# Halves exchanged on ScalarE, and a second layer whose two weight parts pass TensorE as one operand

## The chip, the cores and the metric

The kernel runs on one core of a Trainium2 chip. The time is the device time of one execution in microseconds (us). Three runs of the kernel before gave 2334.14, 2334.78 and 2337.91 us; their median, 2334.78 us, is the time before. One further execution was profiled, and every row quoted below is from that one.

The core's engines are named as the profile names them: PE is TensorE's matmul, PEld its weight load, DVE is VectorE, ACT is ScalarE, POOL is GpSimd, SP is SyncE (here the queue that starts most DMA transfers). PSUM is the memory that PE's matmuls write; the kernel uses it as eight banks of 512 float32 columns each.

## The reference

```python
X = np.fft.rfft(x, axis=1)                       # x: 8 batches, 2496 positions, 256 columns
y = np.fft.irfft(X * F[None], n=2496, axis=1)    # F = filt_r + i filt_i: a global filter
# mixture of experts on the 19968 rows of y: the two best of 8 experts for each row
noisy = x @ w_gate + np.log1p(np.exp(x @ w_noise)) * noise
for e in range(8):
    for k in range(2):                           # rows whose k-th choice is expert e
        h = np.maximum(x[mask] @ w1[e], 0.0)     # 256 -> 1024
        out[mask] += top2_w[mask, k, None] * (h @ w2[e])   # 1024 -> 256
```

Each row passes two experts, so 39936 rows pass the two layers. All of it is float32.

## The kernel before

**The filter.** The transform of a batch is cut into small matrix products (39 by 64 points) over two column halves; `n` counts the halves of all batches, so n = 2 and 3 are the second batch. For each n there are five groups `kg`. `kg1` (line 382 on) multiplies a group by a fixed matrix into a PSUM bank `q3`, and then applies the complex filter: partitions 0 to 63 hold real parts, 64 to 127 imaginary parts. DVE forms `a = p3 * fr` (L397), `b[0:64] = p3[64:128] * fi[64:128]` (L398) and `b[64:128] = p3[0:64] * fi[0:64]` (L399), so the halves change places in the two multiplications that write b. Then a and b are added, on POOL for n below 4 and on DVE afterwards (L400). `kg2` (L413) is the inverse transform of a on PE. The first two batches go through this at the start, in an order that is written out by hand (the list `plan`, kept on each engine by `pin`), together with the gating of the first batch (`gate`, `route`, lines 711 to 925).

**The experts.** `expert` (line 1047 on) works on blocks of 512 rows, four tiles t of 128 rows, and at the end on 18 units of 256 rows, two tiles each. A block belongs to one expert. `gather` fetches its rows from `y` by index (POOL, L977), `turn` transposes them on PE (L993). In the first layer PE computes `hps` for eight slices f of the 1024 hidden columns, ACT applies the relu into `hh` (L1075) and DVE computes the rest, `hl` (L1076). In the second layer PE adds up, for each tile t, the eight slices into `yps`; ACT scales the result by the gate into a row of `stage` (L1100), and POOL adds it to the output by index (L1101).

**Two parts of each number.** After the first stage the operands of matmuls have the type `float32r`, and every operand is split into a high part, rounded to that type, and the rest: weights w1 and w2 in `wsplit` (ACT copies the high part, L1037, DVE subtracts, L1038), activations as `hh` and `hl`. A product then takes three matmuls, which `_mm3` issues at lines 120, 121 and 122: high by high, high by rest, rest by high.

```python
def _mm3(nc, o, lh, ll, rh, rl, start=True, stop=True):
    nc.tensor.matmul(o, lh, rh, start=start, stop=False)
    nc.tensor.matmul(o, lh, rl, start=False, stop=False)
    nc.tensor.matmul(o, ll, rh, start=False, stop=stop)
```

The first operand is loaded into the array (the weight load of PE, 128 by 128), the second streams past it: 512 columns in the first layer, 256 in the second. There the loaded operand is `hh` or `hl`, and the streamed one is `w2h` or `w2l`.

**PSUM.** Of the eight banks two are under the tag `hps`, two under `yps`, one `xps`, three `fps` for the filter. Every third slice of the first layer (f = 2 and 5) uses a `yps` bank too. In the second layer two tiles t share one `yps` bank, each with half of its columns.

**What sets the order.** The order of instructions on each engine is made when the program is built, by a list scheduler that has its own estimate of durations; each engine then runs its list strictly in that order, and semaphores make it wait for the others. `ready` in `expert` is the number of batches whose transform must be complete before a block is taken: the block of batch i has ready = i + 1. From `FIRST` and `PAIRS`, two blocks are taken with ready 1, ten with ready 2 and two with ready 3; all others have ready 4 or more. The filter work of later batches is woven between the blocks.

Of the kernel before, what the change touches and what calls it, by code (L numbers as in the profile page):

```python
# [10 lines left out]
F32 = mybir.dt.float32  # L11
R32 = mybir.dt.float32r
# [3 lines left out]
ALU = mybir.AluOpType  # L16
# [113 lines left out]
PACES = 115  # L130
FILL = {0: 0, 1: 14}
RAW = 3
FIRSTS = 2
EARLY = {"q1": "hps", "q2": "hps", "q5": "yps", "q6": "yps", "u1": "xps"}
BANKS = {"hps": 2, "yps": 2, "xps": 1, "fps": 3}
# [4 lines left out]
class Moe:  # L140
# [165 lines left out]
    def s1(self, bt, g0):  # L306

        nc, P = self.nc, self.P
        if g0 == 0:
            self.Fd[bt] = self.dp.tile([3 * NG, CB, D], F32, name="fd", bufs=2)  # L310
        x = self.xx.pop((bt, g0))
        if self.early and bt < RAW:

            q = self.ps("q1")[:120]
            nc.tensor.matmul(q, self.rC, x, start=True, stop=True)  # L315
            return self.s1e(bt, g0, q)
        xh = P.tile([RP, 512], R32, name="xh", **(dict(tag="w2h", bufs=4) if self.early else dict(bufs=1)))
        xl = P.tile([RP, 512], R32, name="xl", **(dict(tag="w2l", bufs=4) if self.early else dict(bufs=1)))
        nc.scalar.copy(xh, x)
        nc.vector.tensor_sub(xl, x, f32v(xh))  # L320
        q = self.ps("q1")[:120]
        Ch, Cl = self.cC
        nc.tensor.matmul(q, Ch, xh, start=True, stop=False)  # L323
        nc.tensor.matmul(q, Cl, xh, start=False, stop=False)
        nc.tensor.matmul(q, Ch, xl, start=False, stop=True)
        self.s1e(bt, g0, q)
# [54 lines left out]
    def kg1(self, n, kg):  # L381
# [6 lines left out]
        else:  # L388
            nc.tensor.matmul(p, Mh, th, start=True, stop=False)
            nc.tensor.matmul(p, Mh, tl, start=False, stop=False)  # L390
            nc.tensor.matmul(p, Ml, th, start=False, stop=True)
        a = P.tile([128, 4, 128], F32, name="a", **(dict(tag="w2h", bufs=4) if self.early else dict(bufs=2)))
        b = P.tile([128, 4, 128], F32, name="b", **(dict(tag="w2l", bufs=4) if self.early else dict(bufs=1)))
        p3 = p.rearrange("p (k d) -> p k d", k=4)
        fr = self.fr[:, h, 4 * kg:4 * kg + 4]
        fi = self.fi[:, h, 4 * kg:4 * kg + 4]
        nc.vector.tensor_mul(a, p3, fr)  # L397
        nc.vector.tensor_mul(b[0:64], p3[64:128], fi[64:128])  # L398
        nc.vector.tensor_mul(b[64:128], p3[0:64], fi[0:64])  # L399
        (nc.gpsimd if n < 4 else nc.vector).tensor_add(a, a, b)  # L400
        self.zz[n, kg] = a

    def kg2(self, n, kg):
# [627 lines left out]

    def wsplit(self, st, nm, q):
        nc, P = self.nc, self.P
        h = P.tile([128, 2, 256], R32, name=nm + "h", bufs=4)
        l = P.tile([128, 2, 256], R32, name=nm + "l", bufs=4)
        sv = st.rearrange("p (k f) -> p k f", k=2)
        nc.scalar.copy(h, sv)  # L1037
        nc.vector.tensor_sub(l, sv, f32v(h))  # L1038
        return h, l

    def fetch(self, may):

# [5 lines left out]
    def expert(self, parts, may, fill=None):  # L1048
# [5 lines left out]
        while self.ahead:  # L1054
# [33 lines left out]
            yield  # L1088
            for t in range(nt):

                if t % 2 == 0:
                    bank = self.PS.tile([128, 2, D], F32, name="yps", bufs=2)
                p = bank[:, t % 2]
                for f in range(8):
                    h, l = hh[f]
                    wh, wl = w2[f // 2]
                    _mm3(nc, p, h[:, t * 128:(t + 1) * 128], l[:, t * 128:(t + 1) * 128], wh[:, f % 2], wl[:, f % 2],
                         start=(f == 0), stop=(f == 7))
                o = self.slot("yo")
                nc.scalar.activation(o, p, AF.Copy, scale=gate[:, t])  # L1100
                a = nc.gpsimd.indirect_dma_start(  # L1101
                    out=self.io["out"][:BLK + ready * ROWS], out_offset=bass.IndirectOffsetOnAxis(ap=ids[:, t:t + 1], axis=0),
                    in_=o, in_offset=None, compute_op=ALU.add)
# [113 lines left out]
```

## Time and profile before

| | |
|---|---|
| runs | 2334.14, 2334.78, 2337.91 us |
| profiled execution | 2338.18 us, of which the span of its instructions 2336.4 us |
| PE busy | 2282.7 us (98%), 15201 matmuls |
| weight loads busy | 2015.8 us (86%) |
| DVE, ACT, POOL busy | 1442.4 us (62%), 1180.1 us (51%), 942.4 us (40%) |
| DMA | 329.88 MB, mean 141 GB/s |
| granted TensorE clock, mean | 0.993 |

A row of the timeline gives start and duration in us, engine, line, operation, what is written and read, its shape, and how many neighbours it merges; behind it in brackets stands the idle time of the engine before it and what ended that. In a list of groups a row gives the number of instructions, their busy time, the mean of one in ns, and the idle time before them. The end of a matmul is modelled in this profile, so the time of one matmul is read here from the distance between starts, not from its printed duration.

### The profile page before, as it was taken

What the parts mean: (1) busy time and instruction counts of PE and PEld (TensorE: products, weight loads), DVE (VectorE), ACT (ScalarE), POOL (GpSimd) and SP (SyncE); (2) the same over time, 40 slices, a digit from 0 to 9 for tenths busy, and PEclk for the clock granted to TensorE, in tenths of its full rate; (3) what the DMA queues carried; (4) which work ended last, traced back from release to release, by engine and by line L of the source; (5) the groups of instructions that cost most, each with busy time, mean ns of one, the idle gap of its engine ahead of it and who ended that gap; (6) DMA issues with size and microseconds to landing.
All of it is one profiled execution on the core that took longest, in us unless ns stands there. A gap on an engine that the chain in (4) does not pass through costs nothing.

```text
span 2336.4 us, 43304 instructions
## 1 busy us (share of the span) xinstructions
PE 2282.7 (98%) x15201; PEld 2015.8 (86%) x15201; DVE 1442.4 (62%) x3067; ACT 1180.1 (51%) x2353; POOL 942.4 (40%) x837
## 2 busy tenths in 40 slices
PE   8779999999999999999999999999999999999998
PEld 6448888888888888888888888888989898999998
DVE  4967798778669555765558654844343435456775
ACT  6356656654554454444544444444343435456775
POOL 4214244332434333443344333444444444445452
PEclk9989999999999999999999999999999999999999
DMA  8587757765655555455454553344444435567774
GB/s 236 162 244 201 194 139 200 178 157 121 179 133 146 123 123 133 113 145 119 112 118 102 129 140 84 89 99 98 85 94 89 98 84 130 125 162 219 221 224 100
DMA packets 284737, 329.88 MB, mean 141 GB/s; under 512 B 37371, under 2 KB 197603, under 8 KB 284515
## 3 DMA queue, kind: packets, MB, share of 16 engines
q1 hardware_dynamic: 222435, 241.61, 34.5%
q0 software_dynamic: 62080, 85.47, 21.5%
q8 instruction: 121, 1.98, 0.4%
q14 instruction: 101, 0.83, 0.1%
HBM read 221.98 MB, written 105.78 MB: 140 GB/s over the span
## 4 chain that ended last, share of the span: by engine, by line
PE 91%; DVE 4%; DMA 2%; ACT 1%; issue 1%; POOL 0%; SPq 0%; POOLq 0%; ACTq 0%; DVEq 0%
PE yps L122 13%; PE yps L120 13%; PE yps L121 13%; PE hps L120 12%; PE hps L121 12%; PE hps L122 12%; PE xps L993 3%; PE q L413 3%; PE q L477 1%; PE u L424 1%; PE q L500 1%; PE q L315 1%; PE q L502 1%; PE q L501 1%; PE q L323 1%
## 5 line engine op out<-in xcount | busy, mean ns | idle before, releaser
L120 PE MATMUL yps<-w2h,hh 128*128 128x256 f32 x2560 | 725.7, 286 | 0.8 <-ACT stage L1100 0.6
L121 PE MATMUL yps<-w2l,hh 128*128 128x256 f32 x2560 | 716.6, 283 | 0.0
L122 PE MATMUL yps<-w2h,hl 128*128 128x256 f32 x2560 | 706.9, 283 | 0.3 <-DVE hl L1076 0.3
L1076 DVE SCALAR_TENSOR_TENSOR hl<-hps,hh 128x512 fp32r<-128x512 f32 (+1 forms) x712 | 439.1, 631 | 354.1 <-ACT hh L1075 352.7
L1101 POOL DMA_INDIRECT out<-stage,ids x320 | 532.4, 1664 | 202.7 <-ACT stage L1100 127.6
L977 POOL DMA_INDIRECT stage<-y,ids x320 | 323.1, 1010 | 705.3 <-PE xps L993 343.5
L121 PE MATMUL hps<-mxl,w1h 128*128 128x512 f32 (+1 forms) x1424 | 529.4, 373 | 0.0
L122 PE MATMUL hps<-mxh,w1l 128*128 128x512 f32 (+1 forms) x1424 | 526.5, 372 | 0.0
L120 PE MATMUL hps<-mxh,w1h 128*128 128x512 f32 (+1 forms) x1424 | 519.6, 378 | 5.5 <-DVE hl L1076 3.7
L120 PEld LDWEIGHTS yps<-w2h,hh 128*128 128x128 f32 x2560 | 485.7, 190 | 15.1 <-ACT stage L1100 0.8
L122 PEld LDWEIGHTS yps<-w2h,hl 128*128 128x128 f32 x2560 | 482.1, 191 | 11.9 <-issue 1.7
L1075 ACT ACTIVATE hh<-hps 128x512 fp32r<-128x512 f32 (+1 forms) x712 | 382.5, 555 | 216.8 <-PE hps L122 205.3
L121 PEld LDWEIGHTS yps<-w2l,hh 128*128 128x128 f32 x2560 | 485.9, 191 | 6.5
L1100 ACT ACTIVATE stage<-yps,gt 128x256 f32<-128x256 f32 x320 | 147.2, 477 | 330.8 <-PE yps L122 321.1
L122 PEld LDWEIGHTS hps<-mxh,w1l 128*128 128x128 f32 x1424 | 267.4, 188 | 45.8
L120 PEld LDWEIGHTS hps<-mxh,w1h 128*128 128x128 f32 x1424 | 264.6, 189 | 48.8 <-DVE hl L1076 5.9
L121 PEld LDWEIGHTS hps<-mxl,w1h 128*128 128x128 f32 x1424 | 268.0, 188 | 34.7
L998 DVE TENSOR_TENSOR mxl<-xps,mxh 128x512 fp32r<-128x512 f32 (+1 forms) x178 | 113.1, 636 | 145.2 <-ACT mxh L997 142.8
L997 ACT CAST mxh<-xps 128x512 fp32r<-128x512 f32 (+1 forms) x178 | 96.8, 544 | 197.1 <-PE xps L993 163.2
L1038 DVE TENSOR_TENSOR w2l<-stage,w2h 128x512 fp32r<-128x512 f32 x216 | 140.8, 686 | 51.2 <-ACT w2h L1037 48.9
L1037 ACT CAST w1h<-stage 128x512 fp32r<-128x512 f32 x180 | 111.6, 621 | 108.8 <-PE hps L121 70.3
L1038 DVE TENSOR_TENSOR w1l<-stage,w1h 128x512 fp32r<-128x512 f32 x180 | 123.5, 686 | 60.7 <-ACT w1h L1037 57.3
(207 smaller groups left out, 2470.9 us busy)
## 6 DMA issues: line engine op xcount, KB each, us to landing
stage<-w SPq DMA_DIRECT2D x396, 256.0 KB
x<-x SPq DMA_DIRECT2D x88, 256.0 KB
fd<-c SPq DMA_DIRECT2D x77, 240.0 KB
wb<-w SPq DMA_DIRECT2D x18, 1024.0 KB
fx<-fd SPq DMA_DIRECT2D x140, 128.0 KB
out<-z SPq DMA_DIRECT2D x24, 702.0 KB
y<-yt SPq DMA_DIRECT2D x40, 248.6 KB
y<-yt SPq DMA_DIRECT2D x40, 234.0 KB
```

What stands on the lines that cost most here:

```text
L120: nc.tensor.matmul(o, lh, rh, start=start, stop=False)
L121: nc.tensor.matmul(o, lh, rl, start=False, stop=False)
L122: nc.tensor.matmul(o, ll, rh, start=False, stop=stop)
L977: self.pin(lambda: self.nc.gpsimd.indirect_dma_start(out=x, out_offset=None, in_=self.y[:BLK + ready * ROWS], in_offset=bass.IndirectOffse ...
L997: nc.scalar.copy(h, q[:, :w])
L998: nc.vector.tensor_sub(l, q[:, :w], f32v(h))
L1037: nc.scalar.copy(h, sv)
L1038: nc.vector.tensor_sub(l, sv, f32v(h))
L1075: nc.scalar.activation(h, p, AF.Relu)
L1076: nc.vector.scalar_tensor_tensor(l, p, 0.0, f32v(h), op0=ALU.max, op1=ALU.subtract)
L1100: nc.scalar.activation(o, p, AF.Copy, scale=gate[:, t])
L1101: a = nc.gpsimd.indirect_dma_start(out=self.io["out"][:BLK + ready * ROWS], out_offset=bass.IndirectOffsetOnAxis(ap=ids[:, t:t + 1], axis= ...
```

## The change

Two places change, and the buffers of the first stage that go with them.

First, for n = 2 and 3 `kg1` has ACT copy the two halves of the bank crosswise into b (two copies of 64 by 512, L405 and L406 of the changed kernel); DVE then computes a = p3 * fr (L407), b = b * fi over all 128 partitions (L408), and a - b (L409). No addition is left on POOL there.

Second, the high part and the rest of w2 lie in one tile `hl` of shape 128 x 2 x 2 x 256. Where ready is at least 4, one matmul streams both parts past `h`, 512 columns, into a whole bank (L1119), and a second one adds the product of `l` and the high part to its first half (L1120). The second half of the bank is added at the end, by a DVE instruction that multiplies it by the gate and adds it to what ACT has written into `stage` (L1126). Each tile t takes a bank of its own there. Below ready 4 the three matmuls stay.

```diff
+WIDE = 4
@@ s1
-        xh = P.tile([RP, 512], R32, name="xh", **(dict(tag="w2h", bufs=4) if self.early else dict(bufs=1)))
-        xl = P.tile([RP, 512], R32, name="xl", **(dict(tag="w2l", bufs=4) if self.early else dict(bufs=1)))
+        xh = P.tile([RP, 512], R32, name="xh", bufs=1)
+        xl = P.tile([RP, 512], R32, name="xl", bufs=1)
@@ kg1
-        a = P.tile([128, 4, 128], F32, name="a", **(dict(tag="w2h", bufs=4) if self.early else dict(bufs=2)))
-        b = P.tile([128, 4, 128], F32, name="b", **(dict(tag="w2l", bufs=4) if self.early else dict(bufs=1)))
+        if self.early:
+            ab = P.tile([128, 2, 4, 128], F32, name="ab", tag="w2", bufs=4)
+            a, b = ab[:, 0], ab[:, 1]
+        else:
+            a = P.tile([128, 4, 128], F32, name="a", bufs=2)
+            b = P.tile([128, 4, 128], F32, name="b", bufs=1)
...
-        nc.vector.tensor_mul(a, p3, fr)
-        nc.vector.tensor_mul(b[0:64], p3[64:128], fi[64:128])
-        nc.vector.tensor_mul(b[64:128], p3[0:64], fi[0:64])
-        (nc.gpsimd if n < 4 else nc.vector).tensor_add(a, a, b)
+        if 2 <= n < 4:
+            nc.scalar.copy(b[0:64], p3[64:128])
+            nc.scalar.copy(b[64:128], p3[0:64])
+            nc.vector.tensor_mul(a, p3, fr)
+            nc.vector.tensor_mul(b, b, fi)
+            nc.vector.tensor_sub(a, a, b)
+        else:
+            nc.vector.tensor_mul(a, p3, fr)
+            nc.vector.tensor_mul(b[0:64], p3[64:128], fi[64:128])
+            nc.vector.tensor_mul(b[64:128], p3[0:64], fi[0:64])
+            (nc.gpsimd if n < 4 else nc.vector).tensor_add(a, a, b)
@@ wsplit
-        h = P.tile([128, 2, 256], R32, name=nm + "h", bufs=4)
-        l = P.tile([128, 2, 256], R32, name=nm + "l", bufs=4)
+        if nm == "w2":
+            hl = P.tile([128, 2, 2, 256], R32, name="w2", bufs=4)
+            h, l = hl[:, 0], hl[:, 1]
+        else:
+            h = P.tile([128, 2, 256], R32, name=nm + "h", bufs=4)
+            l = P.tile([128, 2, 256], R32, name=nm + "l", bufs=4)
...
-        return h, l
+        return hl if nm == "w2" else (h, l)
@@ expert
-                if t % 2 == 0:
+                wide = ready >= WIDE
+                if wide or t % 2 == 0:
                     bank = self.PS.tile([128, 2, D], F32, name="yps", bufs=2)
-                p = bank[:, t % 2]
+                p = bank[:, 0 if wide else t % 2]
                 for f in range(8):
-                    h, l = hh[f]
-                    wh, wl = w2[f // 2]
-                    _mm3(nc, p, h[:, t * 128:(t + 1) * 128], l[:, t * 128:(t + 1) * 128], wh[:, f % 2], wl[:, f % 2],
-                         start=(f == 0), stop=(f == 7))
+                    h, l = (a[:, t * 128:(t + 1) * 128] for a in hh[f])
+                    hl = w2[f // 2][:, :, f % 2]
+                    if wide:
+                        nc.tensor.matmul(bank, h, hl, start=(f == 0), stop=False)
+                        nc.tensor.matmul(p, l, hl[:, 0], start=False, stop=(f == 7))
+                    else:
+                        _mm3(nc, p, h, l, hl[:, 0], hl[:, 1], start=(f == 0), stop=(f == 7))
                 o = self.slot("yo")
                 nc.scalar.activation(o, p, AF.Copy, scale=gate[:, t])
+                if wide:
+                    nc.vector.scalar_tensor_tensor(o, bank[:, 1], gate[:, t], o, op0=ALU.mult, op1=ALU.add)
```

The lists of the engines move at three places that matter below. In their rows a name with a number is one buffer, and the brackets name the engines whose semaphores the instruction waits for.

PE, a late block of four tiles, at the first matmul of the third tile that it evicts. Before:

```order
L122 MATMUL hps_22100<-mxh1_21971,w1l_21938 128x512
L121 MATMUL hps_22111<-mxl1_21972,w1h_21937 128x512
L122 MATMUL hps_22111<-mxh1_21971,w1l_21938 128x512
L993 MATMUL xps_22204<-ident_70,stage_83 128x128 [waits DMASW4_49,PE_49]
L993 MATMUL xps_22204<-ident_70,stage_83 128x128 [waits DMASW5_49]
L993 MATMUL xps_22204<-ident_70,stage_83 128x128 [waits DMASW6_49]
L993 MATMUL xps_22204<-ident_70,stage_83 128x128 [waits DMASW7_49]
L120 MATMUL yps_21977<-w2h_21615,hh_21834 128x256 [waits Activation_49]
L121 MATMUL yps_21977<-w2l_21616,hh_21834 128x256
L122 MATMUL yps_21977<-w2h_21615,hl_21835 128x256
L120 MATMUL yps_21977<-w2h_21615,hh_21845 128x256
L121 MATMUL yps_21977<-w2l_21616,hh_21845 128x256
```

And with the change, the same place of the same block:

```order
L122 MATMUL hps_20806<-mxh1_20703,w1l_20670 128x512
L121 MATMUL hps_20817<-mxl1_20704,w1h_20669 128x512
L122 MATMUL hps_20817<-mxh1_20703,w1l_20670 128x512
L1007 MATMUL xps_20906<-ident_70,stage_83 128x128 [waits DMASW4_49,PE_49]
L1007 MATMUL xps_20906<-ident_70,stage_83 128x128 [waits DMASW5_49]
L1007 MATMUL xps_20906<-ident_70,stage_83 128x128 [waits DMASW6_49]
L1007 MATMUL xps_20906<-ident_70,stage_83 128x128 [waits DMASW7_49]
L1119 MATMUL yps_20749<-w2_20377,hh_20566 128x512 [waits DVE_49]
L1120 MATMUL yps_20749<-w2_20377,hl_20567 128x256
L1119 MATMUL yps_20749<-w2_20377,hh_20577 128x512
L1120 MATMUL yps_20749<-w2_20377,hl_20578 128x256
L1119 MATMUL yps_20749<-w2_20402,hh_20588 128x512
```

The third tile starts behind the same work. Before, it took the other half of the first tile's bank (yps_21977), and waited for ACT, which had to have read the first half; now it takes the whole bank of the first tile, and waits for DVE, which reads last.

DVE in the same block, before and then with the change:

```order
L1076 SCALAR_TENSOR_TENSOR hl_21912<-hps_21904,hh_21911 128x512 [waits Activation_49]
L998 TENSOR_TENSOR mxl1_21972<-xps_21966,mxh1_21971 128x512 [waits Activation_49]
L1076 SCALAR_TENSOR_TENSOR hl_22108<-hps_22100,hh_22107 128x512 [waits PE_49,Activation_49]
L1076 SCALAR_TENSOR_TENSOR hl_22119<-hps_22111,hh_22118 128x512 [waits PE_49,Activation_49]
L1038 TENSOR_TENSOR w2l_22123<-stage_83,w2h_22122 128x512 [waits DMAHW6_49,Activation_49]
```

```order
L1095 SCALAR_TENSOR_TENSOR hl_20644<-hps_20636,hh_20643 128x512 [waits Activation_49]
L1012 TENSOR_TENSOR mxl1_20704<-xps_20698,mxh1_20703 128x512 [waits Activation_49]
L1126 SCALAR_TENSOR_TENSOR stage_83<-yps_20709,gt_20473,stage_83 128x256 [waits Activation_49]
L1126 SCALAR_TENSOR_TENSOR stage_83<-yps_20729,gt_20473,stage_83 128x256 [waits Activation_49]
L1126 SCALAR_TENSOR_TENSOR stage_83<-yps_20749,gt_20473,stage_83 128x256 [waits Activation_49]
L1095 SCALAR_TENSOR_TENSOR hl_20814<-hps_20806,hh_20813 128x512 [waits PE_49,Activation_49]
L1095 SCALAR_TENSOR_TENSOR hl_20825<-hps_20817,hh_20824 128x512 [waits PE_49,Activation_49]
```

Three of the new additions stand between the rest of the transposed rows (`mxl1`) and the next two `hl`.

DVE at the end of the first stage, at the last group of the second batch. Before, with POOL's addition on its own list, and then with the change:

```order
L397 TENSOR_TENSOR a<-q_1168,fr 128x512 [waits PE_49,Pool_49]
L398 TENSOR_TENSOR b<-q_1168,fi 64x512
L399 TENSOR_TENSOR b<-q_1168,fi 64x512
L902 TENSOR_TENSOR oc<-oc,half 117x224 [waits DVE_49]
L910 TENSOR_TENSOR rx<-rx,ra 128x56 [waits PE_49]
L910 TENSOR_TENSOR rx<-rx,ra 128x56 [waits DVE_49,PE_49]
```

```order
L407 TENSOR_TENSOR ab<-q_1158,fr 128x512 [waits PE_49,Activation_49]
L408 TENSOR_TENSOR ab<-ab,fi 128x512
L924 TENSOR_TENSOR rx<-rx,ra 128x56 [waits PE_49]
L409 TENSOR_TENSOR ab<-ab 128x512 [waits DVE_49]
L924 TENSOR_TENSOR rx<-rx,ra 128x56 [waits DVE_49,PE_49]
```

DVE has three instructions of the group as before, but its first one now waits for ACT's two copies, since all of them write the one tile `ab`.

## The prediction

> **What bounds the kernel now.** I read the page's busy shares first, then the busy time by stretch, then who waits for whom, and last the timeline of PE alone.
>
> ```profile
> PE 2282.7 (98%) x15201; PEld 2015.8 (86%) x15201; DVE 1442.4 (62%) x3067; ACT 1180.1 (51%) x2353; POOL 942.4 (40%) x837
> PE 91%; DVE 4%; DMA 2%; ACT 1%; issue 1%; POOL 0%; SPq 0%; POOLq 0%; ACTq 0%; DVEq 0%
> ```
>
> PE is busy for 98% of the span, and the chain that ended last runs through PE for 91%. The Trainium skill ("Perfetto Trace Analysis", section "Identifying the Most-Contended Engine") says that the busy share of matmuls is a poor measure, since matmuls overlap, and points to the weight loads; these are at 86% here, so the trace agrees that PE is the engine to look at.
>
> A windows view splits the span at the end of the first stage, at the first wide block and at the first small unit. Its columns are the stretch and its length, then busy us and instructions for PE, PEld, DVE, ACT and POOL, granted clock, DMA share and GB/s. The second fence is the list of PE's waits after 622 us (total us, times, longest).
>
> ```profile
> 0.00:200.00 200.00, 162.83 (x868) 106.72 (x869) 138.80 (x408) 101.31 (x200) 51.62 (x55) 0.94 0.73 210
> 622.00:2120.00 1498.00, 1495.92 (x9842) 1336.27 (x9841) 830.21 (x1671) 691.12 (x1337) 628.33 (x547) 1.00 0.50 116
> 2120.00:2336.00 216.00, 206.70 (x1740) 206.23 (x1738) 148.47 (x305) 144.78 (x341) 97.59 (x93) 0.99 0.68 188
> ```
>
> ```profile
> PE hps L120 <- DVE hl L1076: 1.7, 4, 1.0
> PE yps L120 <- ACT stage L1100: 0.6, 1, 0.6
> ```
>
> After 622 us PE waits 2.3 us in all. There the time is what PE needs to issue its list; a shorter list shortens the run one for one as long as no new wait comes. Only the first 200 us, with 37 us of idle PE, are bound by other things.
>
> **What a matmul costs.** Printed durations overlap, so I take the distance between starts. First row and last of a run of first-layer matmuls (512 columns), then of second-layer ones (256 columns):
>
> ```profile
> 2093.09 0.39 PE L120 MATMUL hps<-mxh,w1h 128*128 128x512 f32 x1
> ...
> 2098.43 0.40 PE L122 MATMUL hps<-mxh,w1l 128*128 128x512 f32 x1
> 2324.40 0.28 PE L121 MATMUL yps<-w2l,hh 128*128 128x256 f32 x1
> ...
> 2327.03 0.28 PE L122 MATMUL yps<-w2h,hl 128*128 128x256 f32 x1
> 1806.10 0.28 PE L120 MATMUL yps<-w2h,hh 128*128 128x256 f32 x1
> ...
> 1808.26 0.28 PE L120 MATMUL yps<-w2h,hh 128*128 128x256 f32 x1
> ```
>
> The first run has 23 steps in 5.34 us, 232.2 ns each. The others have 22 steps in 2.63 us and 18 in 2.16 us, 119.5 and 120.0 ns; I use 119.6. Two matmuls of 256 columns take 239.2 ns, one of 512 takes 232.2: what a matmul costs besides its columns is 7.0 ns (6.8 to 7.8 by the two runs). That, and not a third of the work, is what the change can save, because the columns streamed stay the same.
>
> **The change, part by part.** How many are wide: evictions of tiles by stretch, where the kernel's rule puts 56 (14 blocks of four) below ready 4.
>
> ```profile
> 0.00:622.00 622.00, 25.82 (x56) 0.98 0.68 185
> 622.00:2120.00 1498.00, 104.30 (x228) 1.00 0.50 116
> 2120.00:2336.00 216.00, 17.09 (x36) 0.99 0.68 188
> ```
>
> 228 tiles (57 blocks) and 36 (18 units of two) are wide, 264 in all, with eight slices each: 2112 times three matmuls become two. Per slice 3 x 119.6 = 358.8 ns become 232.2 + 119.6 = 351.8. In all 2112 x 7.0 = **14.8 us off PE**.
>
> This prices the wide matmul as a first-layer one of the same width. It differs in one thing that no row shows: its streamed operand is two pieces of 256, 512 elements apart. If a second piece cost what a second matmul costs, it would take 239.2 and PE would gain nothing; at the other end, single steps of that run print as 0.23 or 0.24, so none is below 225 ns, and 2112 x 14.2 ns would be 30 us. I take 232.2, the mean of the nearest rows.
>
> What the additions cost, and the operations of `kg1`:
>
> ```profile
> L1100 ACT ACTIVATE stage<-yps,gt 128x256 f32<-128x256 f32 x320 | 147.2, 477 | 330.8 <-PE yps L122 321.1 <-DMA stage<-y,ids 3.5 <-ACT stage L1100 1.5
> L1076 DVE SCALAR_TENSOR_TENSOR hl<-hps,hh 128x256 fp32r<-128x256 f32 x144 | 57.2, 418 | 18.5 <-ACT hh L1075 18.5
> L397 DVE TENSOR_TENSOR a<-q,fr 128x512 f32<-128x512 f32 x80 | 54.7, 684 | 21.4 <-PE q L391 11.5 <-PE q L387 6.4 <-PE q L349 2.9
> L400 DVE TENSOR_TENSOR a<-a,b 128x512 f32<-128x512 f32 x60 | 41.1, 685 | 0.4
> L400 POOL TENSOR_TENSOR a<-a,b 128x512 f32<-128x512 f32 x20 | 26.1, 1303 | 67.2 <-DVE b L399 50.0 <-DVE st L841 12.1 <-PE q L387 2.6
> L414 ACT COPY G<-q 128x512 f32<-128x512 f32 x80 | 46.9, 587 | 73.1 <-PE q L413 72.7
> ```
>
> A new addition has the form of the 128 x 256 `hl` row, 0.42 us. 264 of them are 110 us of DVE; between 622 and 2120 us they raise it from 830 of 1498 us (55%) to 926 (62%), and the small units from 69% to 76%. DVE stays well below PE, so its total costs nothing. What can cost is the handing over of a bank: the third tile of a block, which waited for ACT, now waits for DVE behind ACT. The same place in the trace:
>
> ```profile
> 1802.53 0.69 DVE L998 TENSOR_TENSOR mxl<-xps,mxh 128x512 fp32r<-128x512 f32 x1 [2.46 <-ACT mxh L997]
> 1803.12 0.84 ACT L1100 ACTIVATE stage<-yps,gt 128x256 f32<-128x256 f32 x2 [0.63 <-PE yps L122]
> 1805.67 0.36 PE L120 MATMUL yps<-w2h,hh 128*128 128x256 f32 x1
> ```
>
> ACT has read the first tile at about 1803.6 (half of the merged row, 0.48). DVE is free since 1803.22, so the addition would end at 1803.6 + 0.05 + 0.42 = 1804.1. PE comes to the third tile at 1805.67, 1.6 us later, and in the new list some 0.23 earlier, since one first-layer matmul less stands between. 1.3 us of cover remain. The fourth tile has more: a tile of 2.8 us lies between. If the cover went, each 1 us of lateness would cost 57 us. I set **1 us** for the new waits, from the places where filter work lies on DVE ahead of an addition; bounds 0 and 15 us.
>
> At the end of the run:
>
> ```profile
> 2324.18 0.38 PE L120 MATMUL yps<-w2h,hh 128*128 128x256 f32 x1 [0.61 <-ACT stage L1100]
> 2327.35 0.47 ACT L1100 ACTIVATE stage<-yps,gt 128x256 f32<-128x256 f32 x1 [3.22 <-PE yps L122]
> 2328.10 1.56 POOL L1101 DMA_INDIRECT out<-stage,ids  x1 [1.95 <-ACT stage L1100]
> ```
>
> The last tile waited 0.61 us for ACT because it shared a bank; with a bank of its own it doesn't: **-0.6 us**. Between the last L1100 and the last L1101 an addition of 0.42 and a handing over of 0.05 come in: **+0.5 us**.
>
> `kg1`, ten groups. DVE has three instructions of 0.68 as before (2.05 us): the multiplication over all partitions takes what L397 or L400 on DVE takes. POOL loses 10 x 1.3 us. ACT gains 20 copies; L414's 0.59 for as many columns is my estimate for each, 12 us, on an engine that is half idle in the first 200 us. On the way of one group POOL's 1.3 us goes away, and ACT's 1.2 us comes ahead of DVE. Which of them shows is told by the last group:
>
> ```profile
> 105.00:115.00 10.00, 8.87 (x63) 5.28 (x64) 9.80 (x22) 2.34 (x5) 3.27 (x3) 0.83 0.23 59
> 112.32 1.10 PE L387 MATMUL q<-fx,cm 128*128 128x512 f32 x2
> 116.51 0.68 DVE L397 TENSOR_TENSOR a<-q,fr 128x512 f32<-128x512 f32 x1
> 118.76 1.27 POOL L400 TENSOR_TENSOR a<-a,b 128x512 f32<-128x512 f32 x1 [3.29 <-DVE b L399]
> 119.74 0.42 PE L913 MATMUL ra<-ident,rx 128*56 128x128 f32 x1 [0.31 <-DVE rx L910]
> 120.08 2.08 PE L413 MATMUL q<-cf,a 128*128 128x128 f32 x8
> ```
>
> DVE is busy 9.80 of 10 us and comes to the group at 116.51, 3 us after its matmul (112.32 plus 1.10): ACT's copies fit in that time. PE stands at L913 until 120.16, which is bound by DVE's `rx`, so POOL's end at 120.03 is not what delays L413. DVE's amount is unchanged, so I take **0**; bounds -1.4 (POOL's leg was the late one after all) and +3 us (DVE meets five of the groups before ACT is done, and waits 0.6 us, one copy, in each).
>
> **Sum.** 2338.2 (the profiled execution) - 14.8 + 1 - 0.6 + 0.5 + 0 = 2324.3. That execution stands 3.4 us above the median of the runs, 2334.78, so for a median of runs I predict 2324.3 - 3.4 = **2321 us**, 0.6% faster. 0.2%, 4.7 us, is about what a measurement of this kernel can tell from no change.
>
> **Rivals.**
>
> A, the wide matmul gains little: its two pieces, or the width itself, cost nearly what a second matmul does. For it speaks that no row has such an operand; against it, that the first-layer matmuls write the same whole bank and load weights just as often. With 236.5 to 239.2 ns per wide matmul PE gains 0 to 5.7 us: 2330 to 2336 us. The Trainium skill ("TensorE: Matmul & The Clock Gate", section "Back-to-back issue gap") gives N / 2.4 GHz plus 2.5 ns as the distance of starts. By that rule a removed matmul saves only 2.5 ns, 5.3 us in all and 2331 us; the trace has 119.6 and 232.2 where the rule has 109 and 216, so I go by the rows.
>
> B, slower: DVE becomes the late one at the third tile. Additions wait in DVE's list for ACT, and everything behind them waits too (`hl`, then PE). It decides from 1.3 us of cover plus 14.8 / 57 = 0.26 us, thus when the addition of a block is 1.6 us late on average, which is two and a half `hl` of 0.69 queued ahead of it. At 2 us late, 57 x 0.7 = 40 us of waits: 2361 us. For it: DVE holds its list strictly in order, and the list was made from estimates. Against: DVE is at 62% there, and PE's wait for `hl` was 1.7 us in 1700 us.
>
> C, more than forecast: a wide step near 225 ns, or the first stage drawing in by 2 us or more: 2305 to 2312 us. The rows give 232 over every long run, so this is unlikely.
>
> **How the numbers follow.** Forecast 0.74, with 2313 to 2329 as its own range (6.8 to 7.8 ns, waits of 0 to 9 us, the first stage -1.4 to +3, and 3 us of scatter between runs). A 0.13, C 0.05, B 0.08. Faster by over 0.2% (below 2330.1): the forecast, C and a sliver of A, 0.80. Within 0.2%: the rest of A, and B where it eats just the gain, 0.13. Slower: 0.07. The range 2312 to 2333 leaves out most of B and C and the end of A, about 0.17.
>
> **What would show it.** Right: 2112 matmuls less (about 13090), wide matmuls at steps of 232 ns and their followers at 120, PE without idle time after 622 us, DVE at 62% between. Wrong: wide steps near 239 (A); waits of yps for DVE L1126 or of hps for `hl` of more than 5 us in all (B); a first wide block that starts more than 3 us away from where it did, which would be `kg1`.

## The result

| | before | after |
|---|---|---|
| median of four runs | 2336.12 us (2334.14 to 2337.91) | 2314.31 us (2312.83 to 2317.03) |
| profiled execution, its span | 2338.18, 2336.4 us | 2317.03, 2315.2 us |
| matmuls in the profile | 15201 | 13089 |

A fourth run of the kernel before, 2337.46 us, moves its median from 2334.78 to 2336.12. The ratio is 0.9905, with a 95% interval of 0.9893 to 0.9916: 0.95% faster, 21.8 us. The prediction was 2321 us with a range of 2312 to 2333, and a gain of about 14 us. The time is inside the range, and about a third of the gain came from a place where I had written 0. Of all runs below one, of the kernel with an idle copy, was slow (4079.99 us at a granted clock of 0.78); it counts in no median and no ratio.

The busy time of the page after, which answers to the first line that the prediction shows:

```profile
PE 2264.9 (98%) x13089; PEld 1898.8 (82%) x13089; DVE 1542.5 (67%) x3331; ACT 1189.4 (51%) x2373; POOL 937.2 (40%) x827
```

The same by stretch (stretch and length, then busy us and instructions of PE, PEld, DVE, ACT and POOL, granted clock, DMA share, GB/s), and behind it PE's waits from 622 us to shortly before the end:

```profile
0.00:200.00 200.00, 166.88 (x916) 110.50 (x917) 132.66 (x418) 117.87 (x231) 45.54 (x52) 0.95 0.76 217
200.00:622.00 422.00, 416.82 (x2741) 365.21 (x2740) 324.24 (x684) 240.69 (x473) 165.16 (x137) 1.00 0.65 171
622.00:2100.00 1478.00, 1477.34 (x8003) 1233.95 (x8003) 921.25 (x1896) 687.69 (x1337) 635.70 (x549) 1.00 0.50 118
```

```profile
PE hps L120 <- DVE hl L1095: 0.7, 3, 0.3
```

PE is as full as before, with about 2100 matmuls less, and waits 0.7 us after 622 us where it waited 2.3. DVE is at 62% between 622 and 2100 us.

**Where the 21 us are.** The evictions of the first tile and of the first wide tile mark the stages. Before, from the timeline of ScalarE:

```profile
195.40 0.84 ACT L1100 ACTIVATE stage<-yps,gt 128x256 f32<-128x256 f32 x2
636.91 0.48 ACT L1100 ACTIVATE stage<-yps,gt 128x256 f32<-128x256 f32 x1
```

After, with the end of the run (the last two tiles' eviction, addition and scatter-adds):

```profile
186.43 0.84 ACT L1124 ACTIVATE stage<-yps,gt 128x256 f32<-128x256 f32 x2
630.39 0.49 ACT L1124 ACTIVATE stage<-yps,gt 128x256 f32<-128x256 f32 x1
2303.83 0.84 ACT L1124 ACTIVATE stage<-yps,gt 128x256 f32<-128x256 f32 x2 [3.50 <-PE yps L1120]
2304.33 0.88 DVE L1126 SCALAR_TENSOR_TENSOR stage<-yps,gt,stage 128x256 f32<-128x256 f32 x2 [3.55 <-ACT stage L1124]
2305.28 1.55 POOL L1127 DMA_INDIRECT out<-stage,ids  x1 [7.90 <-DVE stage L1126]
2307.14 1.56 POOL L1127 DMA_INDIRECT out<-stage,ids  x1 [0.30 <-issue]
```

The first wide tile comes 6.5 us earlier (636.9 to 630.4). The last eviction came at 2327.4 before, as the prediction shows, and comes at 2304.2 now (the second of the merged row): from the first wide tile to the last it is 1690.5 us before and 1673.8 after, 16.7 us less. From the last eviction to the end of the span it was 9.0 us (2336.4 - 2327.4) and is 11.0 us (2315.2 - 2304.2), 2.0 us more. 6.5 + 16.7 - 2.0 = 21.2 us, the difference of the two spans.

**The wide matmul.** From the timeline of PE after, a run of second-layer slices; the first row of the run and its last:

```profile
1800.82 0.28 PE L1120 MATMUL yps<-w,hl 128*128 128x256 f32 x1
1800.94 0.39 PE L1119 MATMUL yps<-w,hh 128*128 128x512 f32 x1
1801.17 0.27 PE L1120 MATMUL yps<-w,hl 128*128 128x256 f32 x1
...
1803.25 0.27 PE L1120 MATMUL yps<-w,hl 128*128 128x256 f32 x1
```

Seven slices in 2.43 us, 347 ns each, where the prediction had 351.8 and the kernel before 358.8. The wide one takes 0.23 us, the narrow one behind it 0.12 and rather less: over all such steps of the trace the median is 232 ns for the wide one and 117 for the narrow one, which was 120 before. Two pieces 512 elements apart cost no more than one piece of 512, so rival A falls.

The gain is not spread evenly. The 57 blocks of four tiles, from the eviction of their first tile to that of their last, take 1461.0 us where they took 1478.1: 17.0 us less, about 9.3 ns for each of 1824 slices, PE's shorter waits included. The small units of two tiles gained nothing: from one to the next it is 11.93 us, and 11.86 before. PE has no wait in the trace there, and what takes the gain back is open.

**The early gain.** Nothing in the forecast explains 6.5 us there. The last but one group of `kg1` of the second batch before, on DVE and POOL:

```profile
111.96 0.68 DVE L397 TENSOR_TENSOR a<-q,fr 128x512 f32<-128x512 f32 x1
112.65 0.69 DVE L398 TENSOR_TENSOR b<-q,fi 64x512 f32<-64x512 f32 x1
113.36 0.68 DVE L399 TENSOR_TENSOR b<-q,fi 64x512 f32<-64x512 f32 x1
114.07 0.28 DVE L901 TENSOR_TENSOR oc<-half,hi 117x224 f16<-117x224 f16 x1
114.21 1.27 POOL L400 TENSOR_TENSOR a<-a,b 128x512 f32<-128x512 f32 x1 [3.66 <-DVE b L399]
114.27 1.50 DVE L903 TENSOR_TENSOR oc<-half,lo 117x512 f16<-117x512 f16 x1
...
115.99 0.41 DVE L903 TENSOR_TENSOR oc<-half,lo 117x512 f16<-117x512 f16 x1
```

The L903 that starts beside POOL's addition lasts 1.50 us and ends shortly after the addition is over (114.21 + 1.27); the next L903, of the same shape, lasts 0.41. The other groups show the same, save the last, where DVE had little left to do. Over the ten groups, what the DVE instructions beside a POOL addition last longer than the shortest of their kind sums to 8.8 us (differences below 0.15 us left out). In the kernel after, no addition of the second batch runs on POOL and the sum is 0. In the first batch, whose additions stay on POOL, nothing is stretched: there DVE runs multiplications that read one operand from PSUM. After, near 27 us:

```profile
26.55 1.26 POOL L414 TENSOR_TENSOR ab<-ab 128x512 f32<-128x512 f32 x1
27.11 0.69 DVE L412 TENSOR_TENSOR ab<-q,fi 64x512 f32<-64x512 f32 x1
```

The Trainium skill ("GPSIMD Engine Reference", section "1. Specifications") says that GpSimd's way into SBUF is shared with VectorE and that VectorE's instructions with two inputs from SBUF, or in a mode that uses two ports, are the ones that contend. The trace agrees: 1.50 against 0.41 us with two inputs from SBUF, 0.69 as ever with one. I had not weighed that rule.

Second, the same three instructions cost DVE less. After:

```profile
108.60 0.67 DVE L407 TENSOR_TENSOR ab<-q,fr 128x512 f32<-128x512 f32 x1
109.20 0.67 DVE L408 TENSOR_TENSOR ab<-ab,fi 128x512 f32<-128x512 f32 x1
109.80 0.19 DVE L924 TENSOR_TENSOR rx<-rx,ra 128x56 f32<-128x56 f32 x1
109.92 0.68 DVE L409 TENSOR_TENSOR ab<-ab 128x512 f32<-128x512 f32 x1
110.52 0.19 DVE L924 TENSOR_TENSOR rx<-rx,ra 128x56 f32<-128x56 f32 x1
```

From start to start L407, L408 and L409 take 0.60 us each, 1.80 in all. L397, L398 and L399 before take 0.69, 0.71 and 0.71, 2.11 in all. The printed durations hide this, since they overlap in the one case and not in the other: 0.31 us per group, 3.1 us for ten. L398 and L399 read half of the partitions and write the other half; the Trainium skill ("VectorE: DVE Perf Modes", section "Two Vector instructions with no wait between them") says, as a model, that an instruction whose operands start in another quarter of the partitions than the last ones in the same memory begins only when all earlier instructions have ended. The distances agree with that; no run here changes the halves alone.

I measure what all of this does to DVE from the first reciprocal of the router (L722 before, L736 after) to the first `ro` (L918, L932). Before:

```profile
63.75 1.25 DVE L722 RECIPROCAL rank<-rank 117x176 f32<-117x176 f32 x1
120.19 0.28 DVE L918 TENSOR_SCALAR ro<-ra 56x128 f32<-56x128 f32 x1 [0.51 <-PE ra L913]
```

After:

```profile
65.07 1.25 DVE L736 RECIPROCAL rank<-rank 117x176 f32<-117x176 f32 x1
111.95 0.28 DVE L932 TENSOR_SCALAR ro<-ra 56x128 f32<-56x128 f32 x1 [1.24 <-PE ra L927]
```

56.4 us before, 46.9 after: 9.6 us less, where the two causes together offer 8.8 + 3.1 = 11.9. I call this the **router stretch** below. By the windows view of this stretch DVE is busy for 53.5 us of it before and for 41.5 after: 12.1 less, so the two causes account for DVE's work. Its idle time grew from 2.9 to 5.4 us, which is the rest.

### The profile page after: what moved, and what is told of

Read it like the earlier page. It is cut to its first block, busy times and chain, and to the rows that moved or that the text cites. A ratio compares the mean times of both kernels' runs of the same rounds, so it can differ in the third digit from the quotient of the medians.

```text
span 2315.2 us, 39310 instructions
## 1 busy us (share of the span) xinstructions
PE 2264.9 (98%) x13089; PEld 1898.8 (82%) x13089; DVE 1542.5 (67%) x3331; ACT 1189.4 (51%) x2373; POOL 937.2 (40%) x827
## 5 line engine op out<-in xcount | busy, mean ns | idle before, releaser
L1119 PE MATMUL yps<-w,hh 128*128 128x512 f32 x2112 | 747.3, 398 | 0.0
L1120 PE MATMUL yps<-w,hl 128*128 128x256 f32 x2112 | 571.3, 281 | 0.0
L991 POOL DMA_INDIRECT stage<-y,ids x320 | 329.6, 1030 | 584.8 <-PE xps L1007 197.6
L121 PE MATMUL hps<-mxl,w1h 128*128 128x512 f32 (+1 forms) x1424 | 535.0, 376 | 0.0
L1119 PEld LDWEIGHTS yps<-w,hh 128*128 128x128 f32 x2112 | 389.3, 188 | 80.2 <-issue 0.2
L1120 PEld LDWEIGHTS yps<-w,hl 128*128 128x128 f32 x2112 | 397.1, 188 | 18.9 <-DVE w1l L1057 0.6
L1126 DVE SCALAR_TENSOR_TENSOR stage<-yps,gt,stage 128x256 f32<-128x256 f32 x264 | 120.9, 479 | 184.6 <-ACT stage L1124 184.2
L963 POOL CAST ids<-lt 128x8 int32<-128x8 f32 (+2 forms) x63 | 15.3, 243 | 379.0 <-DMA lt<-lst 343.8
L1057 DVE TENSOR_TENSOR w<-stage,w 128x512 fp32r<-128x512 f32 x216 | 141.8, 684 | 21.2 <-ACT w L1056 20.8
```

The source lines that it names most:

```text
L991: self.pin(lambda: self.nc.gpsimd.indirect_dma_start(out=x, out_offset=None, in_=self.y[:BLK + ready * ROWS], in_offset=bass.IndirectOffse ...
L1119: nc.tensor.matmul(bank, h, hl, start=(f == 0), stop=False)
L1120: nc.tensor.matmul(p, l, hl[:, 0], start=False, stop=(f == 7))
L1126: nc.vector.scalar_tensor_tensor(o, bank[:, 1], gate[:, t], o, op0=ALU.mult, op1=ALU.add)
```

## The experiments

Theory H: the early gain is DVE's, because POOL's additions no longer hold its instructions (and, in its later form H2, also because three instructions became cheaper). Rival L: it is a latency, POOL's 1.3 us on the way of each group. Rival K: it is not `kg1`'s at all. Ratios are to the kernel before, run beside each. The change has 0.9905 (0.9893 to 0.9916).

**The two parts apart.** `kg1` alone:

```
-WIDE = 4
+WIDE = 99
```

> The change without its second part: no tile of the second layer is wide, kg1's exchange on ScalarE stays. Theory H (a POOL addition of two operands holds DVE's instructions while it runs; ten additions stretch DVE by 8.8 us in the trace of before): the first tile's eviction comes 9 us earlier, the 56th 6.5 us earlier, and since nothing is saved later the time is 2336.1 - 6.5 = 2329.6 us (2328 to 2331). Rival K (the early gain is not kg1's; the wide part brought all 21.8 us, for instance by the shared tile of both weight parts): 2336 us, first eviction near 195.4 us as before.

2328.38 us, ratio 0.9963 (0.9950 to 0.9976). The marks:

```profile
184.84 0.84 ACT L1124 ACTIVATE stage<-yps,gt 128x256 f32<-128x256 f32 x2
629.25 0.48 ACT L1124 ACTIVATE stage<-yps,gt 128x256 f32<-128x256 f32 x1
```

The wide part alone:

```
-        if 2 <= n < 4:
+        if False:
```

> The change without its first part: kg1 as before (three multiplications on DVE, the addition on POOL for the second batch), wide matmuls from four batches on. Theory H: evictions 0 and 56 where they were before (195.4 and 636.9 us), the wide stretch 16.7 us shorter, the end 2.0 us longer: 2336.1 - 14.7 = 2321.4 us (2320 to 2323). Rival K: 2314.3 us as the whole change.

2321.13 us, ratio 0.9930 (0.9917 to 0.9943). The marks:

```profile
193.93 0.84 ACT L1124 ACTIVATE stage<-yps,gt 128x256 f32<-128x256 f32 x2
632.83 0.49 ACT L1124 ACTIVATE stage<-yps,gt 128x256 f32<-128x256 f32 x1
```

Both times lie in the ranges that H gave. `kg1` alone gains 8.6 us (5.6 to 11.7), the wide part alone 16.4 us (13.3 to 19.4); the sum, 25, is above the 21.8 of both, within what the intervals leave. K falls: the early marks move with `kg1`. With the wide part alone the first mark is near its old place, the second 4 us ahead of it; single profiles of kernels with the same early part differ by 1 to 4 us at these marks, so only larger differences count.

**POOL's addition put back, where nobody reads its result.** Behind each subtraction on DVE POOL adds a tile to itself that has been used up:

```
-            nc.vector.tensor_sub(a, a, b)
+            nc.vector.tensor_sub(a, a, b); nc.gpsimd.tensor_add(b, b, b)
```

> The whole change, and behind each of the ten subtractions on DVE one addition on POOL of a tile that nobody reads any more (b becomes b + b), 128 x 512 as before. No other engine has an instruction more or in another order; nothing waits for the result except the buffer. Theory H: the DVE instructions that run beside these ten are stretched again by about 0.9 us each, 8 to 9 us in sum, and the time is 2314.3 + 6.5 to 9 = 2321 to 2323 us; the first eviction is near 195. Rival L (what the change took away was POOL's 1.3 us on the way from a to the next matmul, a latency): POOL's additions lie on nobody's way, 2314.3 us, first eviction near 186.4.

2316.69 us, ratio 0.9915 (0.9903 to 0.9928). The stretching is back:

```profile
97.31 1.04 POOL L409 TENSOR_TENSOR ab<-ab 128x512 f32<-128x512 f32 x1 [1.62 <-DVE tab L883]
97.39 1.09 DVE L915 TENSOR_TENSOR oc<-half,hi 117x224 f16<-117x224 f16 x1
```

L915, of 0.26 us elsewhere, lasts 1.09; the sum is 6.3 us, the router stretch 51.6 us (63.47 to 115.02), 4.7 more than in the change. So the holding is real, and no latency. The time, though, is only 2 us above the change's, within the intervals: I expected 6.5 to 9. The first eviction, at 185.1, did not move either, but it comes from the profiled execution, which at 2312.25 us is the fastest of the six. Holding alone is not the whole early gain.

**Three multiplications and the addition on DVE**, nothing on POOL or ScalarE:

```
-        if 2 <= n < 4:
+        if False:
...
-            (nc.gpsimd if n < 4 else nc.vector).tensor_add(a, a, b)
+            (nc.gpsimd if n < 2 else nc.vector).tensor_add(a, a, b)
```

> The wide part as in the change; kg1 of the second batch without the exchange on ScalarE: three multiplications and the addition all on DVE, none on POOL. DVE gets 10 x 0.685 = 6.9 us more work than in the change, in a stretch where it is 95 to 98% busy, and no stall. Theory H: 6.9 us of work take the place of 8.8 us of stalls: first eviction about 193 us, time 2314.3 + 4.5 to 6.9 = 2319 to 2321 us, 1 to 2 us below the wide part alone. Rival L (POOL's leg was late, DVE's stretched instructions cost nothing): 6.9 us more on the busiest engine, against a leg of 1.3 us less: 2321.4 + 5 = 2326 us or more.

2326.35 us, ratio 0.9954 (0.9941 to 0.9966): the time that L named. The timeline of DVE there:

```profile
112.11 0.69 DVE L412 TENSOR_TENSOR ab<-q,fi 64x512 f32<-64x512 f32 x1
112.82 0.68 DVE L413 TENSOR_TENSOR ab<-q,fi 64x512 f32<-64x512 f32 x1
113.53 0.65 DVE L916 TENSOR_TENSOR oc<-oc,half 117x224 f16<-117x224 f16 x3
114.09 0.68 DVE L414 TENSOR_TENSOR ab<-ab 128x512 f32<-128x512 f32 x1
114.69 0.27 DVE L915 TENSOR_TENSOR oc<-half,hi 117x224 f16<-117x224 f16 x1
```

L412 and L413 take 0.71 us from start to start, L414 takes 0.60, and nothing is stretched. This showed me the second saving: one instruction of 0.60 more and 0.31 of dearer ones make 0.91 us per group, 9.1 for ten, and the router stretch is 56.2 us (63.44 to 119.59), 9.3 above the change's. So DVE's account closes without any latency. Why the run is 5 us slower than the wide part alone, with the same router stretch, is another matter: with DVE's list the order of the matmuls changed too, and between 120 and 640 us PE is busy 497 of 520 us where the wide part alone has 507. The first eviction comes at 202.1 us, 8 us after that of the wide part alone. That the order is what costs this was not tested. So the time of this run does not separate H from L, and my expectation of it was wrong.

**The subtraction on POOL**, the exchange on ScalarE kept:

```
-            nc.vector.tensor_sub(a, a, b)
+            nc.gpsimd.tensor_sub(a, a, b)
```

> The whole change with kg1's subtraction on POOL, as the addition was before: DVE has two instructions per group, ScalarE still exchanges. Theory H2 (the change shortened DVE's list twice: no instruction is held by a POOL addition any more, and three instructions at distances of 0.60 us take the place of three at 0.69 to 0.72 us): DVE loses 10 x 0.60 = 6.0 us and gets 6.3 to 8.8 us of holding back; the stretch from the first reciprocal of the second stage to the first ro is 47 to 50 us (46.9 in the change, 56.5 before), and the time 2314 to 2317 us. Rival L (POOL's leg on the way of a group is what cost): that stretch is back near 56 us and the time near 2321.

2313.82 us, ratio 0.9903 (0.9889 to 0.9917), as the change. POOL's leg is back on the way of every group, and so is the holding:

```profile
104.21 1.36 POOL L409 TENSOR_TENSOR ab<-ab 128x512 f32<-128x512 f32 x1 [1.84 <-DVE G L421]
104.36 1.50 DVE L917 TENSOR_TENSOR oc<-half,lo 117x512 f16<-117x512 f16 x1
```

The stretching sums to 7.9 us, DVE's list is 6.0 us shorter, and the router stretch is 48.5 us (63.69 to 112.22): 46.9 + 7.9 - 6.0 = 48.8. L wanted 56 us and a time near 2321 and falls. What counts is DVE's total, holding included.

**Two idle additions per group, and one idle copy.**

```
-            nc.vector.tensor_sub(a, a, b)
+            nc.vector.tensor_sub(a, a, b); nc.gpsimd.tensor_add(b, b, b); nc.gpsimd.tensor_add(b, b, b)
```

> The whole change, and behind each of the ten subtractions on DVE two additions on POOL of a tile that nobody reads any more (b becomes b + b, twice), where the earlier run had one. Every other engine's list is that of the change. With one addition each, DVE's instructions were stretched by 6.3 us in sum, DVE's stretch from the first reciprocal to the first ro was 51.6 us against 46.9, and the time 2316.7 us. Theory H (a running POOL addition of two operands holds DVE instructions that read two operands from SBUF): about twice the stretching, 12 us, that stretch 56 us as in the kernel before, and about twice the loss of time: 2314.3 + 5 = 2319 us (2317 to 2322). Rival (POOL's work off the way costs nothing, the 2.4 us of the earlier run were scatter between runs): 2314 us.

2323.12 us, where the kernel before, run beside it, has 2339.09: ratio 0.9929 (0.9915 to 0.9943).

```
-            nc.vector.tensor_sub(a, a, b)
+            nc.vector.tensor_sub(a, a, b); nc.gpsimd.tensor_copy(b, b)
```

> The whole change, and behind each of the ten subtractions on DVE one copy on POOL of that tile onto itself: one operand where the addition has two, the same 128 x 512 elements. Theory H1 (what holds DVE is the second operand's reading on POOL): no DVE instruction is stretched, the stretch from the first reciprocal to the first ro is 46.9 us and the time 2314.3. Rival H0 (any POOL pass over a tile holds DVE's two-operand instructions for as long as it runs): they are stretched until the copy ends, by about 5 to 6 us in sum, and that stretch is 51 us or more.

2315.0 us, the median of three runs, ratio 0.9894 (0.9876 to 0.9912). Of the copy's profile:

```profile
68.50 0.61 POOL L409 COPY ab<-ab 128x512 f32<-128x512 f32 x1 [19.55 <-DVE ab L409]
68.61 0.70 DVE L751 TENSOR_TENSOR oh<-gz,m 117x176 f32<-117x176 f32 x1
```

L751 lasts 0.34 us alone and 0.70 here, until shortly after the copy has ended: a POOL instruction with one operand holds DVE too, so H1 falls. H0 is right in kind and wrong in size, because the copy takes POOL only 0.61 us. The four kernels whose lists on PE, DVE, ScalarE and SyncE are the same, and which differ in what POOL does beside them:

| idle work on POOL per group | DVE stretched, us in sum | DVE busy in the router stretch, us | router stretch, us | ratio to before |
|---|---|---|---|---|
| none (the change) | 0 | 41.5 | 46.9 | 0.9905 |
| a copy, 0.61 us | 1.8 | 43.5 | 49.7 | 0.9894 |
| an addition, 1.04 us | 6.3 | 47.4 | 51.6 | 0.9915 |
| two additions | 11.9 | 52.9 | 58.7 | 0.9929 |

DVE's busy time grows as its instructions are stretched, and the 11.9 us of two additions are the 12 that H named. With two additions ScalarE waits once, 2.1 us, for a buffer that POOL still uses, but DVE's idle time, 5.7 us, is close to that of the change, 5.4. The router stretch as a whole is less exact: in the kernel with another order of the matmuls, at the end of this section, whose lists up to there are those of the change, DVE is busy for 41.6 us of it and the stretch is 49.9 us, at a granted clock of 0.90 where the change has 0.96. So the length of the copy's stretch alone tells nothing.

With two additions the loss is 0.0024 x 2336 = 5.6 us, about what H named, for 11.8 us of router stretch; the two intervals only just overlap. The ratio is then that of the wide part alone (0.9930): idle work on POOL has taken back what `kg1` gained, the three cheaper instructions included. The first few microseconds cost nothing that can be measured. That the lateness reaches the end only in part fits `kg1` too: 9.6 us less on DVE, 6.5 us at the first wide tile. The likely reason is that PE waits behind that stretch for other things, for gathered rows above all (from the change's list of PE's waits between 120 and 640 us; total us, times, longest):

```profile
PE xps L1007 <- DMA stage<-y,ids: 8.7, 3, 4.9
```

In the same window this wait is 7.4 to 12.5 us in the eight kernels whose router stretch is below 52 us, and 3.1 to 5.5 in the four where it is above 56, the kernel before among them. That agrees with the reason, but no run changes the gathering alone.

**The end of the run.** The blocks that end a pass keep the old three matmuls; by the counts of the trace (13105 matmuls, 262 additions) these are only the last two tiles of the run:

```
-                wide = ready >= WIDE
+                wide = ready >= WIDE and not late
```

> The whole change, but the blocks that end a pass (after which no block is at hand) keep three matmuls per slice, one shared bank and no addition on DVE, the last two tiles of the run among them. In the trace of the change the last two tiles end together, their two scatter-adds queue on POOL, and the time from the last eviction to the end is 11.0 us against 9.0 before. Theory T (the end is longer because two wide tiles end together): the last stretch is 9.0 us again and the time 2314.3 - 2.0 + 0.3 (a few slices at 8.6 ns more) = 2312.6 us. Rival: the end is as long, since the addition on DVE (0.42 us) and POOL's order are not what lengthens it: 2314.5 us.

2313.30 us, ratio 0.9898 (0.9882 to 0.9914). The end of that run:

```profile
2299.97 1.55 POOL L1127 DMA_INDIRECT out<-stage,ids  x1 [4.91 <-ACT stage L1124]
2302.73 0.47 ACT L1124 ACTIVATE stage<-yps,gt 128x256 f32<-128x256 f32 x1 [3.23 <-PE yps L122]
2303.48 1.55 POOL L1127 DMA_INDIRECT out<-stage,ids  x1 [1.96 <-ACT stage L1124]
```

From the last eviction to the end it is 9.4 us (2312.1 - 2302.7) in place of 11.0: with a bank each, PE's list interleaves the last two tiles, they end together, and their scatter-adds queue. That part of theory T holds in the trace. The run has the lowest median of all, but 1.0 us is less than the intervals can tell from the change.

**All tiles wide.**

```
-WIDE = 4
+WIDE = 0
```

> The whole change, and the first four batches' 56 tiles wide too. From the trace of the change a slice costs 232.8 + 116.5 ns wide and 3 x 119.3 ns narrow, so 56 x 8 x 8.6 ns = 3.9 us come off PE, which is 97 to 99% busy from 200 to 622 us. Theory F (PE's list bounds this stretch as it does the later one): 2314.3 - 3.9 = 2310.4 us. Rival D (DVE, 78% busy there by 324 of 422 us, gets 56 x 0.42 = 23.5 us more and comes late at the third tile of a block, so that PE waits for yps): 2314 us or slower, with waits of yps for the addition above 4 us in the trace.

2334.78 us, ratio 0.9989 (0.9980 to 0.9998): nearly the whole gain is gone, and by neither of the ways I named. PE waits 1.3 us for the addition. PE's idle time lies here, in the windows view of this kernel:

```profile
575.00:600.00 25.00, 20.02 (x134) 15.44 (x129) 20.42 (x59) 10.34 (x23) 8.36 (x6) 1.00 0.60 145
600.00:620.00 20.00, 8.93 (x44) 5.56 (x43) 12.54 (x20) 8.71 (x18) 5.68 (x7) 0.68 0.85 241
```

In these 45 us PE is busy 29.0; in the change it is 42.8. Ahead of the fourth batch's logits the list of PE has 42.3 tiles' worth of second-layer work, where the change has 38.8. The experts' tiles are used up, and the filter of the fourth batch, later by that, runs with nothing beside it (the first `ro` of that batch at 588.0 us, 561.9 in the change). What in the ordering puts the filter back was not tried. These 14 us are most of the 20 that are lost, and the rest was not traced. So below the fourth batch the limit is not PE's list alone.

**Another order of the matmuls**: two wide ones, then their two narrow ones.

```
+                if wide:
+                    for f0 in range(0, 8, 2):
+                        for f in (f0, f0 + 1):
+                            nc.tensor.matmul(bank, hh[f][0][:, t * 128:(t + 1) * 128], w2[f // 2][:, :, f % 2], start=(f == 0), stop=False)
+                        for f in (f0, f0 + 1):
+                            nc.tensor.matmul(p, hh[f][1][:, t * 128:(t + 1) * 128], w2[f // 2][:, 0, f % 2], start=False, stop=(f == 7))
...
```

> The whole change, with the wide tiles' matmuls in another order: two slices' wide ones, then their two narrow ones (wide, wide, narrow, narrow in place of wide, narrow, wide, narrow); the same matmuls and operands. Theory: a matmul of 256 columns takes 116.5 ns only behind a wide one and 119.3 ns behind another of 256 columns, so two slices take 232.8 + 232.2 + 116.5 + 119.3 = 700.8 ns in place of 698.6: 2112 x 1.1 ns = 2.3 us more, 2316.6 us. Rival: the 116.5 ns belong to the second part of the sums (nothing else in their bank), whatever stands ahead: 2314.3 us and 116.5 ns in both places.

2317.15 us, ratio 0.9915 (0.9899 to 0.9932), not to be told from the change. By the starts in its trace a narrow one takes 116 ns (median) when a narrow one follows and 118 when a wide one does. In unbroken runs two slices take 697.8 ns on average where the change has 698.2 (a tenth left out at each end); my theory wanted 2.2 more. So the shorter step does not come from a wide neighbour, and my theory falls, though the time alone, 2317.15, would have fitted it. In the change the narrow tiles of the first batches still take 120 ns. What makes the step shorter in a wide tile stays open.

## Why the prediction was right, and where it was not

- **The bound** held: it is PE's list after 622 us, with 0.7 us of waits, though in the small units the shorter list took no less time.
- **14.8 us off PE**: the count was exact (15201 - 2112 = 13089) and the wide step too (232). The stretch from the first wide tile to the last gained 16.7 us, 7.9 ns per slice in place of 7.0. That the mean is so near is in part luck: the blocks gained 9.3 ns per slice, a narrow step shorter by some 3 ns among it, which I did not foresee, and the small units gained nothing.
- **+1 us for waits at the third tile**: PE has none for the addition between 622 and 2290 us. The 1.3 us of cover were enough everywhere, and rival B did not come.
- **-0.6 and +0.5 at the end**: the wait of 0.6 is gone, and that is counted in the 16.7. The +0.5 was mis-sized: I added 0.47 to a chain of one tile and did not see that banks of their own let the last two tiles end together. From the last eviction to the end it is 2.0 us longer.
- **`kg1`, "DVE's amount is unchanged, so I take 0; bounds -1.4 and +3"**: this step failed. It was worth 6.5 us in the profile and 8.6 (5.6 to 11.7) alone, far beyond the bound of -1.4. I counted DVE's instructions by their printed durations, after having shown for PE that these overlap; and I read the 9.80 of 10 us that DVE was busy as work, while in nine of the ten groups 0.6 to 1.1 us of DVE's busy time was an instruction held by the POOL addition that the change removes. The 10 us that I quoted, from 105 to 115, contained it. In the runs DVE's busy time in the router stretch fell by 12.1 us.
- **The rivals**: A fell with the step of 232 ns. The second half of C, the first stage drawing in by more than 2 us, is what happened; I had given it 0.05 together with a faster wide step, and a time of 2305 to 2312 us, which the 2314.31 misses. The rule from the Trainium skill ("TensorE: Matmul & The Clock Gate", section "Back-to-back issue gap") that I set beside A is stated there for a single matmul by itself, so it was no forecast for a stream of them. With the other terms of the sum it gives 2330.4 us, not 2331. Of the signs that I named, the first wide block more than 3 us away from its place was the one that told.

By terms: 2338.2 - 16.7 - 6.5 + 2.0 = 2317.0, the profiled execution's time. That the time fell inside the range is luck as to `kg1`: its term was outside its own bounds, and only the width of the range as a whole took it in.

## What to carry to other kernels

Where DVE is the full engine, a POOL instruction beside it is not free (here an addition of 1.3 us took 0.6 to 1.1 us of DVE): look on DVE for instructions that last several times as long as their kin and end with a POOL instruction, and count that time as removable from DVE's list. Price DVE's instructions, like PE's, by the distance between starts, not by printed durations. A gain on the engine that bounds one stage need not reach the end in full: here 9.6 us of the router stretch became 6.5 at the first wide tile.

## What the runs showed that I had not expected

- A POOL pass of 128 x 512 f32 holds DVE instructions with two operands from SBUF until it ends (0.41 to 1.50 us, 0.26 to 1.1, 0.34 to 0.70), a one-operand copy on POOL included; DVE instructions with one operand in PSUM run beside it at 0.69 us as ever.
- The same POOL addition takes 1.04 us on one tile added to itself and 1.27 on two tiles.
- On DVE a 64-partition multiplication across halves takes 0.71 us from start to start, a 128-partition one within them 0.60.
- A narrow matmul in a wide tile takes 117 ns, 120 elsewhere; the cause is open.
- The small units of two tiles gain nothing from wide matmuls (11.93 us each, 11.86 before); why is open.
- With wide tiles everywhere 20 of the change's 21.8 us are gone, 14 of them by an idle PE between 575 and 620 us.
